# Scheduler constants of a fused attention and feed-forward kernel, judged by replays with varied lengths instead of the one undisturbed plan

## The chip, the cores and the metric

The kernel runs on one core of a Trainium2 chip. The metric is the device time of one execution in microseconds (us), lower is better. A core has a matrix engine (PE), three engines for elementwise work (DVE, ACT and POOL), and DMA queues; SP issues the transfers here. Each engine works through its own list of instructions in the order in which the program wrote them, and waits where an operand is not ready.

## The reference

Three stages are computed one after another, for 4 batches of 544 tokens and 512 channels:

```
# attention: 8 heads of 64, 512 local tokens and 32 global ones
out_g = softmax(scale * q_g @ [k_g k_l].T) @ [v_g v_l]
s_ll  = where(|i - j| <= 32, scale * q_l @ k_l.T, -1e9)
out_l = softmax([scale * q_l @ k_g.T, s_ll]) @ [v_g v_l]
x = concat(out_g, out_l)                     # (4, 544, 512)
# first feed-forward, 1024 wide
h = relu(x @ w_in)
conv[t] = sum over k of conv_w[k] * h[t + k - 1]     # 3 taps along the tokens
x = (h * sigmoid(conv)) @ w_out
# second feed-forward, 1024 wide
xk = mu_k * x + (1 - mu_k) * x_prev;  xr = mu_r * x + (1 - mu_r) * x_prev
out = sigmoid(xr @ w_r) * (relu(xk @ w_k) ** 2 @ w_v)
```

All data is float32. In the feed-forwards the kernel splits each operand into a high and a low part and makes three products of it (high by high, high by low, low by high).

## The kernel before

**Tiles.** Attention is cut into 16 units u (a batch and a pair of heads). A unit has scores `s` (L541, 32 small matmuls for each of its two heads), a masking pass on DVE that makes `e` (L556), the exponentials on ACT (L563), a transposition `pe` on PE (L572), its copy `eT` (L575), the product with v, `o` (L582), a division on DVE (L592 to L594, tile `xn`), a transposition `X` (L613) and the split into a high and a low `x` (L620, L623). For the global tokens two units go together: `sg` (L665), exponentials `eg` (L682), the normalising of `eg` (fnorm: L697 on ACT, L701 on POOL), the transpositions `peg` (L709), their copies `egT` (L714), the product `Xg` (L724) and its split into `x` (the high part by ACT at L750, the low part by DVE at L753).

The first feed-forward of batch b has two parts, called H and O here. H makes `ph` (L905) in 8 blocks of 128 channels by two halves of the tokens, 12 matmuls each; the first 6 of the 12 need the x of the batch's first two units, the last 6 those of its last two (`x_2`, `x_3` in batch 0). Each block of 128 channels then goes through relu, three taps `c` (L940 to L947), the sigmoid (L953, ACT), the multiplication by h (L956, DVE or POOL) and the split into `gh` (L963) and `gl` (L968). O makes `po` (L1006); its blocks of k come in four pairs, and a pair needs `gh` and `gl` of two blocks of channels: `c_6` and `c_7` are the last pair. The second feed-forward (called moe2 here, with `pk`, `pr` and `pv` on PE) runs in 6 chunks of up to 384 tokens after the last O; its squaring is at L1166.

**What sets the order.** The program first lists all its work as tasks (class Plan), each with an engine, a cost in nanoseconds, its dependencies, the buffers that it takes, and for some a due time, called key. `schedule()` then plays the program through once and writes the instructions in the order that comes out. Of the tasks that can start within WINDOW of the earliest, on the engine of that one, it takes the one with the smallest key. A task that several engines can do goes to the engine with the earliest modelled end, plus a bias for the engine that depends on the modelled time (`bias`, with PHASES as the borders and DVE_BIAS, ACT_BIAS, POOL_BIAS as the values, L386). PENALTY is added to the key of an ACT task that needs another table of functions, AHEAD bounds the bytes under way in DMA, and the FILL constants say where the PE is given empty matmuls (L429) to bridge a wait. The due times come from s_key (L497: T_START and STEP0 for batch 0, T_DENSE, SLOT, LEAD, GAP, GAP1 for the later ones), from the LAG constants (how far behind its unit's start a unit's `pe`, `o`, `X` and `peg` are due), and from d_key (L867: T_DENSE, SLOT, H_FRAC for H and O).

Of the kernel before, what the change touches and what calls it, by code (L numbers as in the profile page):

```python
# [45 lines left out]
W2R_BUFS = 3  # L46
E_STEP = 16
XB = 8
T_START = 3947
STEP0 = 4107  # L50
T_DENSE = 30229
SLOT = 69882
LEAD = -9653
GAP = -8788
GAP1 = 13075
STEPS_H = 6
E_BUFS = 4
H_FRAC = 0.625
LAG_TE = -2476
LAG_PV = 14647  # L60
LAG_G = 12072
LEAD_Q = 6126
S_COST = 880
M_COST = 845
E_COST = 1182
PV_COST = 470
LAG_TX = 18273
WINDOW = 90
FILL_MIN = 31
FILL_MARGIN = 1350  # L70
FILL_START = 6
FILL_RATE = 0.504
PENALTY = 496
AHEAD = 1711
PHASES = (60e3, 105e3, 320e3, 375e3)
DVE_BIAS = (1137, 1116, 682, -803, 690)
ACT_BIAS = (604, 900, -279, 1717, 327)
POOL_BIAS = (914, 623, 302, -621, -2645)
H_BUFS = 5
C_BUFS = 3  # L80
G_BUFS = 4
# [80 lines left out]
class Plan:  # L162
# [50 lines left out]
    def schedule(self):  # L213
# [17 lines left out]
        while cand:  # L231
# [39 lines left out]
            for e, t, o in ests:  # L271
                if o[0] == o0[0] and e <= lim:
                    k = t.key + (PENALTY if t.table and t.table != table else 0)
                    if best is None or k < best[0]:
# [20 lines left out]
            if t.eng == "PE":  # L295
# [4 lines left out]
                unit = 215 / r  # L300
                if t.warm and e - now > FILL_MIN + FILL_MARGIN:
                    n = int((e - now - FILL_MARGIN) / unit)
                    t.fill += n
                    clock.run(now, 215 * n, 1.0, True)
                if t.warm and r == 1.0:
                    left = (k + 1) * Clock.TICK - e
                    lack = Clock.ENOUGH - clock.count.get(k, 0.0) - FILL_RATE * left
                    if lack > 0:
                        n = min(int(lack / (1 - FILL_RATE) / 215) + 1, int(left / 215))
                        t.fill += n  # L310
# [93 lines left out]
def attn_moe_kernel(  # L404
# [92 lines left out]
    def s_key(u):  # L497
        b, s = divmod(u, NP)
        if b == 0:
            return T_START + STEP0 * s  # L500
        g0, gh, g1 = (GAP1 if b == 1 else GAP), H_FRAC * SLOT, SLOT - LEAD
        return T_DENSE + SLOT * (b - 1) + g0 + (g1 - g0) * s / NP

# [23 lines left out]
    def attend(u):  # L527
# [22 lines left out]
        for a in range(2):  # L550
# [36 lines left out]
            def fdiv(a=a, bo=bo):  # L587
                if a == 0:
# [11 lines left out]
            e = add("ACT", E_COST, fe, deps=[m], use=[be], table="exp", name=f"e{u}_{a}")  # L600
            t = add("PE", 437, ft, deps=[e], take=[bp, bt], use=[be], key=k0 + LAG_TE + 1500 * a,
                    name=f"te{u}_{a}", warm=True)
            te = add("ACT", act(512), lambda fev=fev: fev(nc.scalar.copy), deps=[t], use=[bt, bp],
                     name=f"tev{u}_{a}", alts=[("DVE", 600, lambda fev=fev: fev(nc.vector.tensor_copy))])
            pv = add("PE", PV_COST, fpv, deps=[te, ev["v", u]], take=[bo], use=[bt, bufs["v", u]],
                     key=k0 + LAG_PV + 1500 * a, name=f"pv{u}_{a}", warm=True)
            dvs.append(add("DVE", 740, fdiv, deps=[pv] + dvs, take=[bn] if a == 0 else [],
# [6 lines left out]

        tx = add("PE", 437, ftx, deps=dvs, take=[bX], use=[bn], key=k0 + LAG_TX + 1500, name=f"tx{u}")

# [28 lines left out]
    def glob(u):  # L645
# [70 lines left out]
        def fpv():  # L716
            X = alloc(bt[2], [P, 2, SG], F32, f"Xg{u}")
            eT = bT.tile
            for z in range(2):
# [15 lines left out]
                alts=[("ACT", 710, lambda: fnorm(nc.scalar)), ("POOL", 858, lambda: fnorm(nc.gpsimd))])  # L735
        kt = k0 + LAG_G
        evs = []
# [129 lines left out]
    def d_key(b, pos):  # L867
        hp = FT * h_cost
        t0 = T_DENSE + SLOT * b
        if b == B - 1:  # L870
            return t0 + pos
        if pos < hp:
            return t0 + SLOT * H_FRAC * pos / hp
        return t0 + SLOT * (H_FRAC + (1 - H_FRAC) * (pos - hp) / hp)

# [178 lines left out]
    def moe2():  # L1054
        t0 = T_DENSE + SLOT * (B - 1) + 2 * FT * h_cost
        free_out = add("-", 0, alloc_big, deps=[ev["O", B - 1, m, hf] for m in range(KT) for hf in range(2)],
# [234 lines left out]
    wout, wout_done = split_weights("wout", w_out, FT, DM, lambda: woutp, "wo", ("gh", "gl"))  # L1291
    add("DMA", 900, fmus, key=T_DENSE + SLOT * 2, name="mus")
    for b in range(B):
# [113 lines left out]
```

## Time and profile before

| | |
|---|---|
| median of 3 runs | 549.32 us (548.07 to 549.88) |
| the profiled execution | 551.77 us, of which the span of the trace is 550.0 us |
| mean granted clock of PE | 0.988 of full speed |
| busy in the span | PE 528.0, DVE 320.8, ACT 287.0, POOL 155.4 us |

The span runs from the first to the last recorded instruction; the rest of the time lies around it. An engine is busy while one of its instructions runs. PE's two clock levels are 1.2 and 2.4 GHz; a granted clock of 1.00 is the upper one, 0.50 the lower, and a value between them is a mean over a stretch that had both.

### The profile page before, as it was taken

To read this page: it belongs to the slowest core of one execution; us is meant where nothing else is said; L and a number is where in the kernel's file an instruction comes from. 1 tells how busy PE (TensorE), PEld (TensorE's weight loads), DVE (VectorE), ACT (ScalarE), POOL (GpSimd) and SP (SyncE) were. 2 spreads that over 40 slices of the span, in tenths; PEclk is the share of its full clock that TensorE was granted. 3 is DMA by queue.
4 is the path that set the end of the run, shared out by engine and by line. 5 is a ranking of instruction groups with operands and counts; after the bars stand their busy time and mean duration, and the time that the engine had idled before them with its cause. 6 is when DMAs were issued, how large, how long until landed. Compare 5 with 4: busy or idle time off the path is not lost.

```text
span 550.0 us, 13792 instructions
## 1 busy us (share of the span) xinstructions
PE 528.0 (96%) x5498; PEld 483.9 (88%) x5498; DVE 320.8 (58%) x874; ACT 287.0 (52%) x638; POOL 155.4 (28%) x320
## 2 busy tenths in 40 slices
PE   5688989999999999999999999999999999999997
PEld 4576979978999999999999998898898898898896
DVE  4489899176796349942599689998115215111101
ACT  5588988366798559973696574001042142142040
POOL 3053243101021112210100372000089288184060
PEclk9699998999999999999999999999999999999999
DMA  8998854887154670010427532302101100100101
GB/s 262 306 285 287 288 180 152 220 278 246 62 195 124 211 227 6 2 39 25 136 80 216 166 116 72 116 0 59 57 2 38 68 0 21 57 1 0 59 1 38
DMA packets 41088, 64.60 MB, mean 117 GB/s; under 512 B 4928, under 2 KB 31296, under 8 KB 41024
## 3 DMA queue, kind: packets, MB, share of 16 engines
q1 hardware_dynamic: 38720, 59.26, 34.0%
q10 hardware_dynamic: 2304, 4.47, 2.2%
q8 instruction: 43, 0.70, 0.5%
q14 instruction: 21, 0.17, 0.1%
HBM read 51.64 MB, written 12.07 MB: 116 GB/s over the span
## 4 chain that ended last, share of the span: by engine, by line
PE 72%; ACT 1%; DVE 1%; issue 0%
PE pk L1143 17%; PE pv L1246 17%; PE po L1006 13%; PE ph L905 10%; PE pr L1209 9%; PE o L582 1%; PE Xg L724 1%; PE pe L572 1%; PE s L541 1%; PE X L613 1%; PE sg L665 1%; PE peg L709 0%; DVE c L947 0%; ACT c L940 0%; ACT gh L963 0%
## 5 line engine op out<-in xcount | busy, mean ns | idle before, releaser
L905 PE MATMUL ph<-x,win_hi 128*128 128x256 f32 (+1 forms) x512 | 100.4, 294 | 1.3 <-ACT egT L714 0.8
L905 PEld LDWEIGHTS ph<-x,win_hi 128*128 128x128 f32 x512 | 79.9, 188 | 2.9 <-ACT egT L714 1.1
L1006 PE MATMUL po<-gh,wout_hi 128*128 128x256 f32 (+1 forms) x256 | 75.5, 295 | 0.0
L1006 PE MATMUL po<-gl,wout_hi 128*128 128x256 f32 (+1 forms) x256 | 73.9, 289 | 0.1
L1006 PE MATMUL po<-gh,wout_lo 128*128 128x256 f32 (+1 forms) x256 | 73.4, 287 | 0.0
L905 PE MATMUL ph<-x,win_lo 128*128 128x256 f32 (+1 forms) x256 | 73.4, 287 | 0.0
L1143 PE MATMUL pk<-xkl,wkk_hi 128*128 128x384 f32 (+1 forms) x192 | 62.7, 327 | 0.0
L1143 PE MATMUL pk<-xkh,wkk_lo 128*128 128x384 f32 (+1 forms) x192 | 62.7, 327 | 0.0
L1143 PE MATMUL pk<-xkh,wkk_hi 128*128 128x384 f32 (+1 forms) x192 | 62.7, 326 | 0.0
L1166 POOL TENSOR_TENSOR robuf<-robuf 128x384 f32<-128x384 f32 (+1 forms) x40 | 32.9, 824 | 103.1 <-ACT robuf L1161 102.9
L947 DVE SCALAR_TENSOR_TENSOR c<-h,convw,c 128x544 f32<-128x544 f32 x64 | 50.5, 808 | 14.3 <-ACT c L940 12.3
L1246 PE MATMUL pv<-wvv_lo,k2h 128*128 128x512 f32 (+1 forms) x144 | 54.4, 378 | 0.0
L1246 PE MATMUL pv<-wvv_hi,k2h 128*128 128x512 f32 (+1 forms) x144 | 54.4, 378 | 0.0
L1246 PE MATMUL pv<-wvv_hi,k2l 128*128 128x512 f32 (+1 forms) x144 | 54.4, 377 | 0.0
L1161 ACT ACTIVATE robuf<-pk 128x384 f32<-128x384 f32 (+1 forms) x40 | 18.7, 467 | 65.2 <-PE pk L1143 64.5
L1259 DVE TENSOR_TENSOR robuf<-pv,robuf 128x512 f32<-128x512 f32 (+1 forms) x18 | 11.9, 661 | 65.7 <-PE pv L1246 56.6
L1006 PEld LDWEIGHTS po<-gh,wout_hi 128*128 128x128 f32 x256 | 48.2, 188 | 0.3
L1006 PEld LDWEIGHTS po<-gl,wout_hi 128*128 128x128 f32 x256 | 48.2, 188 | 0.3 <-DVE gl L968 0.3
L905 PEld LDWEIGHTS ph<-x,win_lo 128*128 128x128 f32 x256 | 48.2, 188 | 0.0
L1006 PEld LDWEIGHTS po<-gh,wout_lo 128*128 128x128 f32 x256 | 48.2, 188 | 0.0
L563 ACT ACTIVATE e<-e 128x128 f32<-128x128 f32 x128 | 40.2, 390 | 8.4 <-DVE e L556 8.3
L1209 PE MATMUL pr<-wrr_hi,xrbuf 128*128 128x512 f32 x136 | 43.7, 395 | 0.0
(194 smaller groups left out, 1120.6 us busy)
## 6 DMA issues: line engine op xcount, KB each, us to landing
v<-in_v_l_dram SPq DMA_DIRECT2D x16, 910.0 KB, 7.0
kT<-in_k_l_dram SPq DMA_DIRECT2D x16, 336.0 KB, 4.7
qT<-in_q_l_dram SPq DMA_DIRECT2D x16, 288.0 KB, 4.3
x2d<-xo ACTq DMA_DIRECT2D x16, 272.5 KB, 3.5
out_dram<-robuf SPq DMA_DIRECT2D x16, 256.0 KB, 2.0
wout_0r<-in_moe_w_out_dram SPq DMA_DIRECT2D x8, 256.0 KB, 3.8
wkk<-wkkd SPq DMA_DIRECT2D x8, 256.0 KB, 2.9
wout_0r<-in_moe_w_out_dram SPq DMA_DIRECT2D x8, 255.8 KB, 4.3
```

The costliest lines, as they stand in the source:

```text
L541: nc.tensor.matmul(s[a][32 * j : 32 * j + 32, i], lhsT=qT[rows[a], q : q + 32], rhs=kT[rows[a], c : c + P], start=(i == 0), stop=True, ski ...
L563: nc.scalar.activation(be.tile[:, P * i : P * (i + 1)], be.tile[:, P * i : P * (i + 1)], AF.Exp, bias=be.tile[:, SL + i : SL + i + 1], sca ...
L572: nc.tensor.transpose(pt[:, i], be.tile[:, P * i : P * (i + 1)], ident)
L905: nc.tensor.matmul(pm, lhsT=w[:, k, P * m : P * (m + 1)], rhs=x[:, s0:s1], start=(k == 0 and n == 0), stop=(k == KT - 1 and n == 2),)
L947: e.scalar_tensor_tensor(bc.tile, bh.tile[:, k : k + S], convw[:, FT * k + m : FT * k + m + 1], bc.tile, op0=ALU.mult, op1=ALU.add,)
L1006: nc.tensor.matmul(pm, lhsT=w[:, k, P * m : P * (m + 1)], rhs=g[:, k % 2, s0:s1], start=(k == 0 and n == 0), stop=(k == FT - 1 and n == 2),)
L1143: nc.tensor.matmul(bp.tile[:, :n], lhsT=w[:, k, P * m : P * (m + 1)], rhs=x[:, :n], start=(k == 0 and i == 0), stop=(k == KT - 1 and i == 2),)
L1161: e.activation(kk()[:, :n], bp.tile[:, :n], AF.Relu)
L1166: e.tensor_mul(ks()[:, :n], kk()[:, :n], kk()[:, :n])
L1209: nc.tensor.matmul(bp.tile, lhsT=x[:, P * j : P * (j + 1)], rhs=w[:, k], start=(k == 0 and i == 0), stop=(k == KT - 1 and i == 2),)
L1246: nc.tensor.matmul(bp.tile, lhsT=x, rhs=w[:, k, c0:c1], start=(k == 0 and i == 0), stop=(k == FT - 1 and i == 2),)
L1259: nc.vector.tensor_mul(o()[:, c0:c1], bp.tile, r()[:, c0:c1])
```

## The change

Only numbers are changed: the constants above get new values. The functions that use them, the tasks, their costs and their dependencies stay as they were. The new values were picked by a search that replays each order with varied lengths of the tasks; the old ones had been picked by the single plan that `schedule()` makes.

```diff
-T_START = 3947
-T_DENSE = 30229
+T_START = -1763
+T_DENSE = 17832
...
-LAG_PV = 14647
-LAG_G = 12072
+LAG_PV = 43495
+LAG_G = 2385
...
-PENALTY = 496
+PENALTY = 1220
-PHASES = (60e3, 105e3, 320e3, 375e3)
-DVE_BIAS = (1137, 1116, 682, -803, 690)
+PHASES = (45588, 264400, 484313, 683508)
+DVE_BIAS = (1064, 1001, -4113, 2464, 14683)
```

The same lines change in the same manner for STEP0, SLOT, LEAD, GAP, GAP1, H_FRAC, LAG_TE, LEAD_Q, LAG_TX, FILL_MIN, FILL_MARGIN, FILL_RATE, AHEAD, ACT_BIAS and POOL_BIAS.

**What it does to the program.** The matmuls are the same ones, in another order, but for one empty matmul that is no longer there. Of the tasks that have a choice of engine, these change theirs: 14 of the 32 multiplications by h go from DVE to POOL, all but one of them in batches 1 to 3; 32 of the 48 squarings of moe2 go from POOL to DVE, with 24 of its subtractions for the low part of the square; 12 low parts of weights (win and the weight wvv of moe2) go from POOL to DVE. The orders of PE and of the queue of loads are the same up to the first 46 rows of PE. After that the q and k of units 4 to 6 are loaded ahead of the last two tiles of w_in (columns 512 and up, k of 2 and 3).

On ACT, ahead of the high parts of `x_2` and `x_3` that the second half of batch 0's H needs, there stood before:

```order
L790 CAST convm<-convr 128x24
L843 CAST win_hi<-win_512m 128x512
L714 COPY egT_858<-peg_1_904 128x384
L563 ACTIVATE e_0_912<-e_0_912 128x128 x4
L790 CAST wout_0m<-wout_0r 128x512
L563 ACTIVATE e_1_964<-e_1_964 128x128 x4
L750 CAST x_2_166<-Xg_969 128x32
L750 CAST x_3_168<-Xg_969 128x32
```

And now, on the same engine and at the same place:

```order
L790 CAST convm<-convr 128x24
L843 CAST win_hi<-win_512m 128x512 x2
L563 ACTIVATE e_1_955<-e_1_955 128x128 x4
L790 CAST wout_0m<-wout_0r 128x512
L563 ACTIVATE e_0_980<-e_0_980 128x128 x4
L563 ACTIVATE e_1_986<-e_1_986 128x128 x4
L843 CAST wout_hi<-wout_0m 128x512
L682 ACTIVATE eg_1029<-sg_0_968,eg_1029 128x480
L682 ACTIVATE eg_1029<-sg_1_969,eg_1029 128x64
L750 CAST x_2_166<-Xg_998 128x32
L750 CAST x_3_168<-Xg_998 128x32
```

Counted from ACT's first row, two more sets of exponentials of a unit (`e`, one of them ahead of the rows shown), one more cast of wout, one more copy `eT` and the exponentials of the next pair's global tokens (`eg`) now stand ahead of the two casts.

The normalising of batch 1's first `eg` stood on ACT, behind three sigmoids of batch 0's gate:

```order
L575 COPY eT_0_1409<-pe_0_1388 128x512
L953 ACT_TABLE_LOAD
L953 ACTIVATE c_4_1359<-c_4_1359 128x544
L953 ACTIVATE c_3_1375<-c_3_1375 128x544
L953 ACTIVATE c_6_1399<-c_6_1399 128x544
L697 ACTIVATE eg_1063<-eg_1063 128x608
L963 CAST gh_4_1508<-c_4_1359 128x544
```

It stands on POOL now, among the clearings of the buffers for wout and ahead of the first h of batch 0:

```order
L785 MEMSET wout_0m 128x512
L525 MEMSET v_951 128x28
L672 MEMSET eg_1029 128x64
L785 MEMSET wout_0m 128x512 x2
L701 TENSOR_SCALAR eg_1029<-eg_1029 128x608
L785 MEMSET wout_0m 128x512
L925 MEMSET h_0_1096 128x1
```

So it comes before all sigmoids, on another engine.

Around the sigmoid of `c_7`, the last block that batch 0's O waits for, ACT had this order:

```order
L714 COPY egT_1525<-peg_1_1593 128x384
L953 ACTIVATE c_5_1591<-c_5_1591 128x544
L953 ACTIVATE c_7_1599<-c_7_1599 128x544
L790 CAST ewkk_0m<-ewkk_0r 128x256
L563 ACT_TABLE_LOAD
L563 ACTIVATE e_0_1631<-e_0_1631 128x128 x4
```

Now it has this one:

```order
L953 ACTIVATE c_5_1482<-c_5_1482 128x544
L714 COPY egT_1504<-peg_1_1565 128x384
L563 ACT_TABLE_LOAD
L563 ACTIVATE e_0_1596<-e_0_1596 128x128 x4
L953 ACT_TABLE_LOAD
L953 ACTIVATE c_7_1570<-c_7_1570 128x544
L750 CAST x_4_172<-Xg_1620 128x32
L750 CAST x_5_174<-Xg_1620 128x32
```

A set of exponentials, with a load of the table for them and one back, has moved in between the two sigmoids. On PE, batch 0's O now has all four groups of `po` on its third pair, and then the scores of two units, ahead of the first `po` on the last pair; before, it had two groups and the scores of one unit there, and the scores of the other unit came after O.

## Rows read from the trace of the kernel before

**Rows 1.** The page, part 1 (busy us, share, instructions) and part 2 (40 slices).

```profile
PE 528.0 (96%) x5498; PEld 483.9 (88%) x5498; DVE 320.8 (58%) x874; ACT 287.0 (52%) x638; POOL 155.4 (28%) x320
...
PEclk9699998999999999999999999999999999999999
```

**Rows 2.** Windows: stretch, length, busy PE PEld DVE ACT POOL, PEclk, DMA share, GB/s.

```profile
40.00:74.00 34.00, 31.78 (x392) 29.52 (x391) 30.73 (x84) 31.86 (x71) 7.74 (x26) 1.00 0.91 301
...
151.00:311.50 160.50, 160.28 (x1966) 155.05 (x1966) 112.30 (x310) 114.60 (x238) 21.59 (x82) 1.00 0.38 117
311.50:550.00 238.50, 235.16 (x1213) 210.59 (x1211) 101.18 (x196) 63.92 (x146) 96.42 (x120) 1.00 0.14 44
```

**Rows 3.** The chain that ended last, in order of time, two pieces of batch 3.

```profile
263.11 24.31 PE ph L905 x192
287.42 24.11 PE po L1006 x192
```

**Rows 4.** Timeline of PE at batch 0's second half of H (start, us).

```profile
50.17 0.63 PE L572 MATMUL pe<-ident,e 128*128 128x128 f32 x4 [0.29 <-DVE e L556]
...
52.68 0.50 PE L905 MATMUL ph<-x,win_hi 128*128 128x256 f32 x2
```

**Rows 5.** Timeline of ACT ahead of that point.

```profile
46.12 0.22 ACT L790 CAST convm<-convr 128x24 f16<-128x24 bf16 x1 [1.54 <-POOL v L525]
...
47.13 1.28 ACT L563 ACTIVATE e<-e 128x128 f32<-128x128 f32 x4
...
50.11 0.25 ACT L750 CAST x<-Xg 128x32 fp32r<-128x32 f32 x2
50.66 0.62 ACT L843 CAST wout_hi<-wout_0m 128x512 fp32r<-128x512 f32 x1 [0.30 <-DVE wout_0m L794]
```

**Rows 6.** Timeline of DVE at the same point.

```profile
51.39 0.27 DVE L753 TENSOR_TENSOR x<-Xg,x 128x32 fp32r<-128x32 f32 x2
```

**Rows 7.** Timeline of PE in batch 0's O.

```profile
81.81 0.55 PE L709 MATMUL peg<-ident,eg 128*128 128x128 f32 x3 [1.91 <-ACT eg L697]
...
91.04 1.16 PE L541 MATMUL s<-kT,qT 64*32 64x128 f32 x64
...
92.54 0.36 PE L1006 MATMUL po<-gh,wout_hi 128*128 128x256 f32 x1
```

**Rows 8.** Windows in batch 0's O and right behind it (columns as in rows 2).

```profile
82.00:87.00 5.00, 5.00 (x111) 4.11 (x111) 4.70 (x10) 4.03 (x8) 2.10 (x3) 0.66 0.34 110
100.00:104.00 4.00, 4.00 (x34) 4.00 (x33) 0.00 (x0) 0.00 (x0) 0.00 (x0) 1.00 0.80 232
```

**Rows 9.** Timeline of ACT in batch 0's O.

```profile
80.97 0.79 ACT L697 ACTIVATE eg<-eg 128x608 f32<-128x608 f32 x1
...
87.81 1.36 ACT L953 ACTIVATE c<-c 128x544 f32<-128x544 f32 x2 [0.72 <-DVE c L947]
...
89.57 1.28 ACT L563 ACT_TABLE_LOAD   x1
```

**Rows 10.** Timeline of POOL in batch 0's O.

```profile
88.61 2.25 POOL L956 TENSOR_TENSOR c<-c,h 128x544 f32<-128x544 f32 x2 [2.55 <-ACT c L953]
```

**Rows 11.** Timeline of DVE in batch 0's O.

```profile
90.82 0.79 DVE L963 CAST gh<-c 128x544 fp32r<-128x544 f32 x2
91.52 1.35 DVE L968 TENSOR_TENSOR gl<-c,gh 128x544 fp32r<-128x544 f32 x2
```

**Rows 12.** Timeline of PE in batch 1's attention and first H.

```profile
115.45 1.84 PE L572 MATMUL pe<-ident,e 128*128 128x128 f32 x8
...
126.44 0.53 PE L905 MATMUL ph<-x,win_hi 128*128 128x288 f32 x2 [0.82 <-ACT egT L714]
```

**Rows 13.** Timeline of DVE, the division behind an `o` (last operation).

```profile
37.93 0.42 DVE L594 TENSOR_TENSOR xn<-o,xn 128x256 f32<-128x256 f32 x1
```

**Rows 14.** A group of DVE by line and form (busy, mean ns, idle before).

```profile
L1166 DVE TENSOR_TENSOR robuf<-robuf 128x384 f32<-128x384 f32 x8 | 4.5, 557 | 0.2
```

More of the change, by code (lines that the diff above doesn't have):

```diff
@@ L48 @@
 XB = 8
-T_START = 3947
-STEP0 = 4107
-T_DENSE = 30229
[L52 to L55, printed above, removed]
+T_START = -1763
+STEP0 = 4043
+T_DENSE = 17832
+SLOT = 73969
+LEAD = -12026
+GAP = -1608
+GAP1 = 16095
 STEPS_H = 6
 E_BUFS = 4
-H_FRAC = 0.625
-LAG_TE = -2476
-LAG_PV = 14647
-LAG_G = 12072
-LEAD_Q = 6126
+H_FRAC = 0.649
+LAG_TE = -2867
+LAG_PV = 43495
+LAG_G = 2385
+LEAD_Q = 2184
 S_COST = 880
@@ L66 @@
 PV_COST = 470
-LAG_TX = 18273
+LAG_TX = 30701
 WINDOW = 90
-FILL_MIN = 31
-FILL_MARGIN = 1350
+FILL_MIN = 695
+FILL_MARGIN = 3342
 FILL_START = 6
-FILL_RATE = 0.504
-PENALTY = 496
-AHEAD = 1711
-PHASES = (60e3, 105e3, 320e3, 375e3)
-DVE_BIAS = (1137, 1116, 682, -803, 690)
-ACT_BIAS = (604, 900, -279, 1717, 327)
-POOL_BIAS = (914, 623, 302, -621, -2645)
+FILL_RATE = 0.433
+PENALTY = 1220
+AHEAD = 1768
+PHASES = (45588, 264400, 484313, 683508)
+DVE_BIAS = (1064, 1001, -4113, 2464, 14683)
+ACT_BIAS = (490, 169, -8356, -6555, -2690)
+POOL_BIAS = (4492, 476, -3056, -5498, 6560)
 H_BUFS = 5
```

## The prediction

> **What bounds the kernel now.** I read the page first. PE is busy in 528.0 of 550.0 us, and the work of PE is the same before and after but for one empty matmul [rows 1]. So the end can move only by the time that PE loses: where it waits, and where its clock is granted at the lower level. The row of the granted clock shows where to look: it falls below the highest digit in some slices of the first 110 us and nowhere behind them [rows 1].
>
> Next I cut the span into windows. From 151.0 to 311.5 PE is busy in 160.28 of 160.5 us at a clock of 1.00: nothing is to be gained there, only lost. From 311.5 to the end it is busy in 235.16 of 238.5, and DVE in 101.18 [rows 2]. The chain of waits in order of time agrees: a whole H takes 24.31 us and a whole O 24.11, each 192 matmuls back to back, 0.126 us apiece [rows 3]. That leaves the front. The order of PE and of the loads is unchanged over the first 46 rows of PE, so what is lost before some 31 us stays lost. From 40 to 74 us PE has 2.2 us of idle time, and its feeders are nearly full: DVE is busy in 30.73 and ACT in 31.86 of 34 us [rows 2]. There, in batch 0's O, and in batch 1's attention the change can do something. I take these places in order of time. All sums are made against the profiled execution (551.77 us, span 550.0), which lies 2.45 us above the median of 549.32; I apply the difference to the median.
>
> **Place 1, batch 0's second half of H: +1.3 us.** Before, PE began it at 52.68 [rows 4]. Its inputs are two casts by ACT that began at 50.11 and ended at 50.36 [rows 5], and two subtractions by DVE behind them, which ended at 51.39 + 0.27 = 51.66 [rows 6]. So the inputs were there 1.02 us before PE came. Now ACT has more ahead of the two casts: two sets of exponentials of 1.28 busy each, one cast of wout of 0.62 [rows 5], and the exponentials of `eg`, 544 columns in two instructions, which by the 512 columns of a set I put at 1.1. That is 4.3 by busy times; neighbours overlap by about 0.1 at each seam (the casts that began at 50.11 were ended 0.30 before the next began at 50.66), so I count 3.9. The copy `eT` and what else moved I put into ACT's remaining idle time: 34 less 31.86 is 2.1, of which 1.54 is one wait, ahead of the cast of the conv weights [rows 2, 5], and 0.6 is left. That wait of 1.54 goes too, because the cast stands behind more work now. So the inputs come 3.9 − 1.54 = 2.4 later, PE's slack of 1.02 takes its part, and 1.3 is left: H's second half begins near 54.0. Bounds: if all 2.1 of idle time, and the 0.30 at 50.66, are filled, 3.9 − 2.4 − 1.0 = +0.5; if none is, because the loads are late, 3.9 − 1.0 = +2.9. The loads: q and k of units 4 to 6, 1.25 MB, go ahead of two tiles of w_in, which at the 301 GB/s of that stretch [rows 2] makes these some 4.1 us late. The tiles themselves are needed only 72 matmuls (9 us) into the second half, which hides that; without the cover the 4.1 us would stand in H. Of the 12 low parts of weights that go from POOL to DVE, four are w_in's and fall here; DVE's own idle time of 3.3 us [rows 2] is their cover, and if it did not hold, the low parts of x would be late by as much as ACT's and not on top of it.
>
> **Place 2, batch 0's O: −2.6 us.** Before, PE waited 1.91 us for ACT's normalising of `eg`, until 81.81 [rows 7]. ACT had it behind three sigmoids, at 80.97 [rows 9]. Right after, PE's mean clock from 82 to 87 was 0.66 [rows 8]: 3.4 of the 5 us at the lower level, where half of the work is lost, 1.7 us. The normalising is now on POOL and far ahead, so 1.91 + 1.7 = 3.6 can be saved. Against this stands the last pair of O. Before, the sigmoid of `c_7` ended at 87.81 + 1.36 = 89.17, POOL's multiplication at 90.86 [rows 9, 10], `gh` and `gl` on DVE at 91.52 + 1.35 = 92.87 [rows 11], while PE came at 92.54 [rows 7]: just in time. Now two loads of tables (1.28 each [rows 9]) and a set of exponentials (1.2) stand ahead of that sigmoid, 3.8 us; the normalising that left ACT gives back 0.8. The sigmoid ends near 92.2, and with a multiplication of 1.12, a `gh` of 0.4, a `gl` of 0.68 and half a microsecond of hand-overs the pair is there at 94.9. When does PE come? Before it took 92.54 − 52.68 = 39.9, of which 3.6 are the loss above: 36.3. Now 12 more `po` (1.5) and one more block of scores (1.16 [rows 7]) stand ahead of the pair; the four transpositions more and four fewer that go with them cancel. So 54.0 + 36.3 + 2.7 = 92.9 or so. The wait is at most about 2.0, and none if `c_5` and `c_7` come earlier through H, whose order also changed. I take half, 1.0, and 2.6 of the 3.6 are saved. Bounds: −3.6 without a wait, and +0.1 if the wait of 2.0 is followed by the same 1.7 us of low clock.
>
> **Place 3, batch 1's attention: −0.9 us.** Eight transpositions took 1.84 us where four back to back are 0.44, so 0.96 is a pause within them, and PE waited 0.82 at 126.44 for a copy [rows 12]: 1.8 together. The scores of the third unit now stand inside O, so its exponentials can run around 100 us, where DVE, ACT and POOL have no work at all [rows 8]. I take half; bounds 0 and −1.8.
>
> **Place 4, the start of the third H: +0.4 us.** A transposition `X` now stands six `po` (0.75 us) behind its `o`. Between them lies DVE's division, whose largest operation is 0.42 [rows 13]; with two small ones ahead and two hand-overs it is about 1.1. Bounds 0 and +1.0.
>
> **The rest, 0.** The 13 multiplications that go to POOL in batches 1 to 3 lie where DVE is busy in 112.30 of 160.5, ACT in 114.60 and POOL in 21.59, and PE never waits [rows 2]; without that cover a multiplication on POOL costs 0.4 us more than one on DVE. In moe2 DVE gets 32 squarings of 0.557 [rows 14] and 24 subtractions of the like, about 31 us on 101.18 of 238.5 [rows 2]: 133, still far below PE. Bounds 0 and +1.0 (a chunk that starts with one of these).
>
> **The sum**: 1.3 − 2.6 − 0.9 + 0.4 = −1.8. The span would be 548.2 and the median 549.32 − 1.8 = **547.5 us**. 0.3%, about what a measurement here can tell from no change, is 1.65 us.
>
> **Rivals.**
>
> *A larger gain.* No wait for the last pair, all of place 3, the low bound at place 1: 0.5 − 3.6 − 1.8 = −4.9, 544.4 us. For it speaks that DVE has less ahead of `c_7`; against it that place 1 is late by ACT's plain work.
>
> *The low clock moves to place 1.* In the trace a wait of 1.91 us at 79.9 was followed by 3.4 us at a granted clock of half [rows 7, 8]. Now the last transposition of `e` ahead of H's second half ends near 50.80 as before [rows 4] (the scores of `sg`, which stood behind it, have moved ahead of it and end by then if their inputs let them), and H goes on at 54.0: a pause of up to 3 us, longer than the one that was followed by the low clock. That costs 1.7 once more: −0.1, 549.2 us. The Trainium skill ("TensorE: Matmul & The Clock Gate", Part 1, The HAM clock gate) says that the throttled clock is the default and activity releases it; by that rule this pause costs a stretch of half clock just as the other did, and the sum would be this rival's. The trace bears it out at 82 us; at 50 us, with a pause of 0.29 [rows 4], the clock stayed at 1.00 [rows 2].
>
> *Slower: ACT's queue.* If ACT is late by all that was put ahead of H's second half (+2.9), `c_7` is late with it; the pair's wait then comes in full with its low clock (+0.1), nothing is won at place 3, and +0.4 stays: +3.4, 552.7 us. It decides from the point where the casts of `x_2` and `x_3` end after 54 us. For it speaks that ACT is the fuller of the two feeders, against it that much of that work could start earlier than its old place.
>
> *The terms cancel otherwise* (place 3 not won, the pair's wait in full without the low clock): 1.3 − 1.6 + 0.4 = +0.1, 549.4 us.
>
> **Chances.** The forecast, −1.7 to −4, 0.32; the larger gain 0.13: faster 0.45. The low clock at place 1 0.20 and the terms that cancel 0.12: same 0.32. Slower 0.23. Forecast and larger gain start at 543.5; of the slower cases the upper part, above 551.5, is left out with some 0.1, and below 543.5 another 0.08. The forecast's own range is 545.3 to 547.6.
>
> **What the changed profile would show.** Right: `ph` on `x_2` begins near 54.0 and ACT's two casts end near 52.7; the wait of 1.91 for the normalising is gone and the granted clock from 80 to 88 is 1.00; the wait for the last pair is below 2 us; less idle time between 115 and 128; windows from 151 on as full as before. Wrong: a granted clock near 0.5 right behind 54 us, a wait ahead of the last pair that is followed by one, new waits in batches 1 to 3 for POOL's multiplications, or gaps of PE in moe2 behind DVE.

## The result and the profile after

The change makes the kernel slower: 552.66 us median of 10 runs, against 548.54 for the kernel before in 10 runs beside them. The ratio is 1.0078, with a 95% interval of 1.0055 to 1.0101, so some 4.3 us (3.0 to 5.5). The forecast of 547.5 us had the wrong sign, and its range ended at 551.5. The profiled execution took 553.6 us, with a span of 551.8.

The page of the changed kernel, parts 1 and 2 (to be held against [rows 1]):

```profile
PE 525.0 (95%) x5496; PEld 483.1 (88%) x5496; DVE 330.5 (60%) x911; ACT 306.3 (56%) x678; POOL 84.3 (15%) x241
...
PEclk9798999999999999999999999999999999999999
```

POOL has lost almost half of its work and ACT and DVE have it, on average with much room. Averages don't show where it hurts; windows of the changed kernel do (columns as in [rows 2]):

```profile
40.00:74.00 34.00, 26.41 (x319) 24.25 (x304) 25.77 (x73) 28.55 (x67) 10.13 (x29) 0.90 0.90 300
46.00:50.40 4.40, 2.01 (x53) 1.87 (x54) 3.42 (x25) 2.12 (x6) 0.58 (x2) 1.00 1.02 329
50.40:51.20 0.80, 0.80 (x4) 0.44 (x3) 0.51 (x1) 0.80 (x4) 0.00 (x0) 0.51 0.75 235
54.00:58.00 4.00, 3.83 (x20) 3.83 (x21) 2.24 (x7) 2.95 (x11) 1.85 (x7) 0.59 0.78 265
...
151.00:311.50 160.50, 159.87 (x2079) 154.66 (x2079) 113.89 (x294) 112.56 (x234) 29.97 (x89) 1.00 0.37 115
313.50:552.00 238.50, 235.03 (x1213) 210.45 (x1211) 113.14 (x244) 82.94 (x184) 17.08 (x31) 1.00 0.14 44
```

From 151 on PE is as full as it was, and moe2 takes the same time although DVE has 113.14 us of work in it where it had 101.18 [rows 2]. What is lost is lost ahead of that: in the first window PE is busy in 26.41 of 34 us, where it was 31.78, and the granted clock is 0.90. The clock falls at 50.4: up to there it is 1.00, though from 46.0 on PE is busy in only 2.01 of 4.40 us, and right behind it is 0.51. The timeline of PE in the changed kernel shows at which instructions (start, duration, instruction, and in brackets the idle time ahead of it with what ended it):

```profile
43.03 1.16 PE L541 MATMUL s<-kT,qT 64*32 64x128 f32 x64 [1.49 <-ACT egT L714]
...
46.50 0.34 PE L665 MATMUL sg<-kT,qT 128*64 128x64 f32 x4 [1.23 <-DVE e L556]
48.72 1.59 PE L724 MATMUL Xg<-egT,v 96*64 96x32 f32 x48 [1.89 <-DVE e L556]
...
54.17 1.11 PE L572 MATMUL pe<-ident,e 128*128 128x128 f32 x4 [2.93 <-ACT eg L682]
54.94 0.77 PE L905 MATMUL ph<-x,win_hi 128*128 128x256 f32 x2
...
78.48 0.39 PE L1006 MATMUL po<-gl,wout_hi 128*128 128x256 f32 x1 [0.68 <-DVE gl L968]
...
95.62 1.95 PE L541 MATMUL s<-kT,qT 64*32 64x128 f32 x119
99.81 0.43 PE L541 MATMUL s<-kT,qT 64*32 64x128 f32 x9 [2.24 <-issue]
100.16 0.39 PE L1006 MATMUL po<-gh,wout_hi 128*128 128x256 f32 x1
...
128.98 1.24 PE L724 MATMUL Xg<-egT,v 96*64 96x32 f32 x36 [1.08 <-ACT egT L714]
```

The second half of batch 0's H begins at 54.94 (before 52.68 [rows 4]). The wait of 1.91 us for the normalising [rows 7] is gone, as predicted. New are waits of 1.49, 1.23 and 1.89 us between 41 and 49, a pause of 2.93 us ahead of that H, one of 2.24 us inside a block of scores, and a wait at 128.98 for the copy that PE had waited 0.82 us for [rows 12]. The waits of 1.23 and 1.89 belong to one change of PE's order: the scores `sg` of the next pair, which stood behind the transpositions `pe`, now stand ahead of `Xg`, and both wait there for DVE's `e`, the pass that reads the scores before them.

### The profile page after: what moved, and what is told of

It is laid out like the page before. It is cut to its first block, busy times and chain, and to the rows that moved or that the text cites. A ratio compares the mean times of both kernels' runs of the same rounds, so it can differ in the third digit from the quotient of the medians.

```text
span 551.8 us, 13735 instructions
## 1 busy us (share of the span) xinstructions
PE 525.0 (95%) x5496; PEld 483.1 (88%) x5496; DVE 330.5 (60%) x911; ACT 306.3 (56%) x678; POOL 84.3 (15%) x241
## 4 chain that ended last, share of the span: by engine, by line
PE 77%; DVE 4%; DMA 3%; ACT 2%; issue 1%; POOL 1%; ACTq 0%; DVEq 0%; SPq 0%; POOLq 0%
PE pk L1143 17%; PE pv L1246 17%; PE po L1006 15%; PE ph L905 11%; PE pr L1209 9%; PE s L541 2%; PE Xg L724 2%; PE o L582 2%; PE pe L572 1%; DVE c L947 1%; DMA ewkk_0r<-in_moe_w_k_dram 1%; DMA wkkd<-ewkk_768m 1%; DMA ewkk_512r<-in_moe_w_k_dram 1%; PE X L613 1%; DMA wkkd<-ewkk_256m 1%
## 5 line engine op out<-in xcount | busy, mean ns | idle before, releaser
L905 PE MATMUL ph<-x,win_lo 128*128 128x288 f32 (+1 forms) x256 | 73.8, 288 | 0.0
L1161 ACT ACTIVATE robuf<-pk 128x384 f32<-128x384 f32 (+1 forms) x48 | 22.7, 473 | 74.8 <-PE pk L1143 74.7
L947 DVE SCALAR_TENSOR_TENSOR c<-h,convw,c 128x544 f32<-128x544 f32 x64 | 53.1, 844 | 11.9 <-ACT c L940 9.6
L956 POOL TENSOR_TENSOR c<-c,h 128x544 f32<-128x544 f32 x23 | 27.8, 1214 | 66.2 <-ACT c L953 66.2
```

The source lines that it names most:

```text
L905: nc.tensor.matmul(pm, lhsT=w[:, k, P * m : P * (m + 1)], rhs=x[:, s0:s1], start=(k == 0 and n == 0), stop=(k == KT - 1 and n == 2),)
L947: e.scalar_tensor_tensor(bc.tile, bh.tile[:, k : k + S], convw[:, FT * k + m : FT * k + m + 1], bc.tile, op0=ALU.mult, op1=ALU.add,)
L956: e.tensor_mul(bc.tile, bc.tile, bh.tile[:, 1 : S + 1])
L1161: e.activation(kk()[:, :n], bp.tile[:, :n], AF.Relu)
```

## The experiments

Ratios are to the kernel before, run on the same chip beside each kernel. In the diffs, `put(names, behind)` takes tasks out of the finished order and puts them right behind another task, and `fn = opts[0]` or `opts[1]` sets a task's operation to its form for ACT or DVE (`opts[2]`, for the normalising, to the one for POOL). A line of dots stands for lines left out of a diff: those that set behind which transfer a moved load may start. No kernel here leaves out work.

**Each kernel looked at twice more.** The first question was whether one profile of each is enough. Both were run again unchanged, two executions of each with a profile.

> The kernel before, unchanged, for a second profile. Single executions of one kernel have differed by 5 to 8 us so far, more than the two kernels do, so the places have to be compared over several profiles. Theory A: the spread arises in the first 33 us (loads and clock), and from the first global product to the second half of H batch 0 takes 16.6 to 16.9 us as in both profiles of this order so far. Rival B: the spread arises everywhere, and the two profiles so far agree by chance.

> The kernel before once more, as its second profile: theory A has the span follow the time at which the first global product starts, within 1.5 us; rival B has it not follow.

> The changed kernel, unchanged, for a second profile. Theory A (the loss is at fixed places): from the first global product to the second half of batch 0's H takes 20 us or more, against 17 in the kernel before, and the pause of 2.2 us inside the second of two blocks of scores stands ahead of O's last pair again. Rival B: either is gone, and was an accident of one execution.

> The changed kernel once more: theory A has the second half of H at 20 us or more behind the first global product and the pause between the scores at 2 us; rival B has at least one of them away.

They took 546.71 and 547.95 us (before), 556.96 and 555.73 us (after). The timeline of PE in the first of these executions of the kernel before:

```profile
51.86 0.50 PE L905 MATMUL ph<-x,win_hi 128*128 128x256 f32 x2
...
74.75 0.38 PE L1006 MATMUL po<-gl,wout_hi 128*128 128x256 f32 x1 [0.63 <-DVE gl L968]
...
79.84 0.55 PE L709 MATMUL peg<-ident,eg 128*128 128x128 f32 x3 [0.20 <-ACT eg L697]
```

And in the second:

```profile
52.20 0.50 PE L905 MATMUL ph<-x,win_hi 128*128 128x256 f32 x2
...
80.19 0.55 PE L709 MATMUL peg<-ident,eg 128*128 128x128 f32 x3 [0.21 <-ACT eg L697]
```

From the first `Xg` to H's second half it took 17.4 and 16.2 us in the kernel before (16.6 to 16.9 had been expected) and 19.7 and 19.8 in the changed one (20 or more). The span did not follow the start of that `Xg`: 35.83, 34.44 and 36.02 us go with spans of 550.0, 544.9 and 546.2.

In neither execution of the kernel before does PE wait 1.91 us for the normalising: it waits 0.20 and 0.21, and the clock stays up. The 3.6 us that the forecast wanted to save at its place 2 were an accident of the one execution that was read. The new pauses are no accident as a whole, though each varies. Here is the window from 40 to 140 us of the first of those two executions of the kernel before:

```profile
40.00:140.00 100.00, 97.40 (x1465) 90.44 (x1465) 76.12 (x246) 79.21 (x183) 23.11 (x77) 0.99 0.73 236
```

The same window of the second:

```profile
40.00:140.00 100.00, 95.92 (x1459) 88.40 (x1458) 75.89 (x244) 78.45 (x181) 23.12 (x77) 1.00 0.72 237
```

And the same window of the changed kernel in its second execution:

```profile
40.00:140.00 100.00, 90.06 (x1376) 83.46 (x1376) 69.38 (x224) 73.46 (x172) 24.63 (x71) 0.93 0.71 228
```

The third:

```profile
40.00:140.00 100.00, 91.16 (x1382) 85.04 (x1382) 69.07 (x225) 74.51 (x175) 24.13 (x71) 0.93 0.70 226
```

PE is idle some 5 to 7 us longer and runs at a granted clock of 0.93 where it was 0.99 to 1.00. The starts of batch 0's second H and of moe2 cut the span in three. That H begins at 52.25 on average over the three executions of before and at 54.93 after: +2.7. From there to moe2 it is 256.3 (254.6 to 258.9) and 260.4 (258.6 to 261.8): +4.1. Moe2 itself is the same. The sum of 6.8 is above the 4.3 us of the medians because all three profiled executions of the changed kernel were above its median: their spans are 551.8, 555.2 and 554.0, and the median of 552.66, less the 1.8 us outside the span, is 550.9.

Two of the new waits come every time: those for DVE's `e` at `sg` (1.11 to 1.24 us) and at `Xg` (1.88 or 1.89) stand in all eleven profiles of the changed order and its variants, and ahead of `Xg` in none of the nine of the old order. In all eleven the granted clock falls around them, between 46 and 51 us, and stays down for 3.4 to 10.2 us. No experiment here put `sg` back, so what this costs is not shown.

**The normalising on POOL, alone, in the kernel before.** This takes the one part of the change that the forecast counted as its gain.

```diff
+put(["gi5", "gn5"], "gl0_1")
+task["gn5"].fn = task["gn5"].opts[2][2]
```

> The kernel before with the normalising of batch 1's first eg, and the two small operations of DVE ahead of it, put before three taps of the convolution and onto POOL: the part of the change from which the prediction took its gain, alone. Theory A (prediction, place 2): PE's wait of 1.91 at 79.9 and the 3.4 us of half clock behind it go, 3.6 us, 545 where the kernel before has 548.5. Rival B: the pause goes, but PE then comes earlier to the next transposition or to the last pair and waits there (PE came just in time for that pair): between -0.5 and -2 us.

548.96 us, 1.0022 (0.9992 to 1.0051): no gain. The timeline of PE:

```profile
78.82 0.52 PE L709 MATMUL peg<-ident,eg 128*128 128x128 f32 x3 [1.08 <-DVE xn L592]
```

Counted from H's second half, the transposition begins at 28.9 us, against 29.1, 28.0 and 28.0 in the three executions of the kernel before; PE now waits there for an operation of DVE on `xn`. The first theory, that the change wins place 2 and loses it elsewhere, falls: there was next to nothing to win.

**Scores apart.** In the changed order two blocks of 64 score matmuls stand behind each other in batch 0's O. Here the second goes 24 `po` further back, as in the order before.

```diff
+put(["s8"], "O0_1_1.3")
+put(["m8_0"], "s8")
```

> The changed kernel with the scores of the second of the two units that stand back to back ahead of O's last pair put 24 matmuls of that pair later. Theory A (PE's pause of 2.24 us inside the second of these two blocks, which the profile puts to no wait, is PE getting its instructions: two blocks of 64 small matmuls in a row use them up faster than they are fetched): the pause is gone, and the time falls by about 2.2 us against the changed kernel, to 550.4. Rival B (PE waits there for the last pair or for a buffer): the pause stands at the same time, ahead of the last pair, and the time stays within 0.7 us.

549.93 us, 1.0038 (1.0008 to 1.0067): it takes back about half of the loss. The two blocks run without a pause:

```profile
94.55 1.16 PE L541 MATMUL s<-kT,qT 64*32 64x128 f32 x64
...
98.85 1.16 PE L541 MATMUL s<-kT,qT 64*32 64x128 f32 x64
```

What stopped PE in the changed kernel has no semaphore: the releaser is "issue", in the middle of a block. The view of the DMA queues from 95.0 to 97.5 us says what else went on (packets, MB, time as a share of the 16 engines'):

```profile
q1 hardware_dynamic: 526, 0.94, 101.2%
```

And from 97.5 to 100.0:

```profile
q1 hardware_dynamic: 308, 0.43, 51.7%
q8 instruction: 1, 0.02, 2.5%
```

Queue q8 is taken to be that of PE's instructions: its 43 packets of 16 KB are 64 bytes for each of PE's 10,992 recorded operations, weight loads included. Its only packet in this stretch was on its way from 97.58 to 98.56, PE stood still from 97.57 to 99.81, and loads of v and of tiles of w_k had filled all DMA engines until then. The same pause is 1.67 us in the second execution, ahead of the very same matmul, where the packet landed at 97.15 and PE stood from 97.10 to 98.78; it is missing in the third, where all 128 matmuls take 2.06 us and the packet had landed 1.99 us before PE came to that matmul. With the scores apart it had landed 2.69 us before, with the DMA engines as full (103.8% from 92.0 to 95.6 us). That the scores' place costs the pause is shown, and the rows tie it to the packet (the last section has more of them); that the packet was late because of the loads is argued, for no run took the loads away.

The converse, the two blocks together in the kernel before:

```diff
+put(["s7"], "s8")
```

> The kernel before with the scores of a second unit put right behind those of another in batch 0's O, as the changed kernel has them. Theory A (two blocks of 64 small matmuls in a row outrun the fetching of PE's instructions): a pause of 1.5 to 2.5 us appears inside or right behind the second block that no wait explains, and 549 to 550 where the kernel before has 547.5. Rival B (the pause belongs to what else is ready there): no such pause, and a time within 0.7 us.

551.66 us, 1.0076 (1.0047 to 1.0104), some 4 us. The timeline of PE in it:

```profile
91.98 1.08 PE L541 MATMUL s<-kT,qT 64*32 64x128 f32 x56 [2.44 <-DVE e L556]
```

The window of this kernel from there on:

```profile
92.00:97.00 5.00, 5.00 (x76) 4.80 (x77) 1.91 (x12) 1.93 (x7) 0.30 (x3) 0.66 0.65 234
```

Here the pause has another releaser: the second block waits for DVE's `e`, the operation that reads scores. Then comes a stretch at 0.66. So the neighbours cost time in either order, but not by one mechanism.

**ACT's cast of wout, later.** In the changed kernel the timeline of ACT ahead of batch 0's second H reads:

```profile
49.88 0.77 ACT L790 CAST wout_0m<-wout_0r 128x512 f16<-128x512 bf16 x1 [2.28 <-DMA wout_0r<-in_moe_w_out_dram]
50.52 2.44 ACT L563 ACTIVATE e<-e 128x128 f32<-128x128 f32 x8
...
54.31 0.26 ACT L750 CAST x<-Xg 128x32 fp32r<-128x32 f32 x2
```

The cast waits 2.28 us for its load, and two sets of exponentials, those of `eg` and the casts of `x_2` and `x_3` stand behind it. The first run moves the cast and its three successors behind the next pair's `eg`; the second joins this with the scores apart.

```diff
+put(["abswout0_0", "lowwout0_0", "hiwout0_0", "lowout0_0"], "gi5")
```

> The changed kernel with one thing put elsewhere: the four operations on the first tile of wout (cast on ACT, low bits on DVE, high and low part) stand behind the split of batch 0's second global product instead of ahead of two sets of exponentials. Theory A (the cast waits 2.3 us for its load at the head of ACT's list and holds up everything behind it): ACT's wait of 2.28 at 49.9 is gone, H's second half begins near 52.5 instead of 54.94, the pause of 2.9 us ahead of it shrinks below 1 us and with it the stretch of half clock at 54 to 57: 2.4 + up to 1.2 us, 549 to 550.5 where the changed kernel has 552.7. Rival B (ACT's plain amount of work is what is late, not the wait): the second half begins at 54 or later, and the time stays within 1 us of the changed kernel's.

> The changed kernel with both moves, the first wout tile later and the two blocks of scores apart. If both theories hold, their gains add, since the places lie 40 us apart with PE never idle for long between them: 552.7 - 3.5 - 2.2 = 547.0, which is 1.5 us below the kernel before. If the gains do not add (the time won at the first place is waited away at the last pair, whose c_7 is not earlier): 549 to 550.

553.14 us, 1.0115 (1.007 to 1.0159), and 553.99 us, 1.0116 (1.0077 to 1.0155). H's second half begins at 51.10 in the first, 3.8 us earlier (3.3 counted from batch 0's fourth block of scores), and nothing is won. The timeline of PE in that first one:

```profile
77.08 0.58 PE L1006 MATMUL po<-gl,wout_hi 128*128 128x256 f32 x1 [3.10 <-DVE gl L968]
```

The window of the same kernel around it:

```profile
76.00:83.00 7.00, 5.92 (x36) 5.57 (x40) 5.02 (x7) 4.62 (x10) 3.56 (x5) 0.51 0.12 39
```

What PE gained it now waits for at O's fifth `po`, the first that needs the low part of the second of the first pair's two blocks: that pair of gated blocks is not there sooner. A limit that neither theory had named holds batch 0 together.

**What makes O's first pair late?** Counted from batch 0's fourth block of scores, that `po` begins 56.8, 57.6 and 56.8 us later in the three executions of the kernel before and 56.0 in its variant with POOL, but 60.8, 59.1 and 61.6 in those of the changed kernel (where PE waits for it 0.68, 0 and 2.39 us) and 59.9 in its variant with the later cast. The timeline of ACT shows the delay on its way, in the sigmoids of the first three blocks. In the kernel before:

```profile
64.59 0.66 ACT L953 ACTIVATE c<-c 128x544 f32<-128x544 f32 x1
...
66.25 0.66 ACT L953 ACTIVATE c<-c 128x544 f32<-128x544 f32 x1
```

In the changed kernel:

```profile
64.91 0.66 ACT L953 ACTIVATE c<-c 128x544 f32<-128x544 f32 x1
...
71.06 0.67 ACT L953 ACTIVATE c<-c 128x544 f32<-128x544 f32 x1
```

The first of them is that of the pair's first block and the third that of its second. Between them ACT had two operations of relu besides a sigmoid; now it has eleven others, among them two casts of wout and two first taps. No run put this order of ACT back. Two suspects were tested: the load of v of unit 5 (910 KB), now ahead of wout's tiles, and eight operations that went from DVE to ACT in that stretch (three casts for wout, three relu, two copies). First each is undone in the changed kernel, alone and with the scores apart, and then both.

```diff
 # wout first
+put(["ldwout1_0", "ldwout2_0", "ldwout3_0", "ldv5"], "ldwout0_0")
+put(["one5"], "zerowout4_0")
 ...
 # eight on DVE
+for n in ["hiwout1_0", "hiwout4_0", "hiwout6_0", "relu0_6_0",
+          "relu0_6_1", "relu0_5_0", "tev4_1", "tev5_1"]:
+    task[n].fn = task[n].opts[1][2]
```

> The changed kernel with the loads of three tiles of wout ahead of the load of v for unit 5 (910 KB), and the clearing of that v later on POOL. Theory A (ACT's cast of wout waits for its load because v's load shares the queues with it, and in order behind it stand the exponentials and the split that H's second half needs; moving the cast alone only put the wait at O's first pair, because wout's later casts then held up the relu of H): the cast's wait is below 0.5 us, H's second half begins within 35 us of the fourth block of scores (37.2, 36.2 and 36.5 in the three profiles of the changed kernel, 33.9 to 34.8 in those of the kernel before), no wait for gl above 1 us follows at O's first pair, and the time falls by 1.5 to 3 us from 552.7. Rival B (ACT's plain work): the wait goes, but the second half still begins 36 us or more behind, and the time stays within 1 us.

> The same, and the two blocks of scores apart as in the earlier run that gave 549.9. Theory A: both gains add to 547 to 548, the level of the kernel before (547.5 on that chip); this would account for the whole loss. Rival B: 549.5 or more, some loss is elsewhere.

> The changed kernel with eight operations of batch 0's H back on DVE, where the kernel before has them: three high parts of wout, three relu, two copies eT (1.3 + 1.2 + 1.3 us of DVE for about 4.0 of ACT); nothing is moved. Theory A (ACT is the engine that is too full in H: from 64 to 72 us it is busy in 7.99 of 8 us there, and DVE waits for it, 7.3 us in all between 46 and 80, against 2.1 in the kernel before): DVE's waits for ACT halve, gl of O's first pair is there 2 to 4 us earlier counted from the fourth block of scores (60 to 61.6 us now, 56 to 57.8 in the kernel before), and the time falls by 1.5 to 3 us from 552.7. Rival B (wout's late loads are what is late in H): gl stays within 1 us of where it is, and so does the time.

> The same eight operations back on DVE, and the two blocks of scores apart (549.9 alone). Theory A: the two places account for the loss, so 547 to 548.5, the level of the kernel before (547.5 to 548.5). Rival B: no better than 549.5.

> The changed kernel with three things set back together: six of wout's loads ahead of v of unit 5 and of q and k (as the kernel before has them), the eight operations on DVE, and the two blocks of scores apart. Theory A (loads and engine choice make the first pair of O late only together: with either alone the other still holds it up): gl of that pair within 58 us of the fourth block of scores, and a time at the level of the kernel before, 547 to 549. Rival B (it is the order of the operations on ACT and DVE in H that is worse): gl at 60 or later and 550 or more.

Wout first: 554.14 us, 1.0117 (1.0074 to 1.0161), and with the scores apart 552.0, 1.0071 (1.0045 to 1.0098). Eight on DVE: 554.75, 1.0134 (1.0105 to 1.0163), and with the scores apart 551.41, 1.0058 (1.0036 to 1.008). All three, with all of wout's first seven tiles ahead of v: 554.99, 1.0131 (1.01 to 1.0162). Neither suspect, undone here, gives anything back; the scores apart help each time (by 0.45% and 0.75%; only together with the later cast they did not). The timeline of ACT with wout first shows why:

```profile
46.67 0.76 ACT L790 CAST wout_0m<-wout_0r 128x512 f16<-128x512 bf16 x1 [0.53 <-DMA wout_0r<-in_moe_w_out_dram]
...
58.96 0.78 ACT L790 CAST wout_0m<-wout_0r 128x512 f16<-128x512 bf16 x1 [3.93 <-DMA wout_0r<-in_moe_w_out_dram]
```

The wait of 2.28 has moved: 0.53 us for the first tile, 3.93 for a later one. With all three it is 6.02 us at wout's last tile. With the eight on DVE, the list of ACT's waits from 46 to 80 us has one that has grown from 1.0 us in the changed kernel (us in total, times, longest):

```profile
ACT c L940 <- DVE gl L968: 3.8, 2, 2.5
```

So in these rows one part put back alone makes another wait longer.

**The same suspects, added to the kernel before.** There the surroundings are the old ones.

```diff
 # eight on ACT: as above with opts[0]
 # v early
+put(["ldv5"], "ldwout0_0")
 ...
 # scores together
+put(["s7"], "s8")
```

> The converse: the kernel before with the same eight operations put on ACT, nothing moved. Theory A: gl of O's first pair comes 2 to 4 us later, PE waits for it 2 us or more where it waits 0.6, and the time rises by 1.5 to 4 us. Rival B: no more than 0.7 us, DVE and ACT are exchangeable there.

> The kernel before with the load of v for unit 5 (910 KB) right behind the first tile of wout, where the changed kernel has it, nothing else moved: the converse for the loads. Theory A: ACT's casts of wout then wait for their loads, 2 us or more in all, gl of O's first pair comes 1 to 3 us later, and the time rises by 1 to 3 us. Rival B: within 0.7 us, the loads have slack in this order.

> The kernel before with both things that make O's first pair late there: the load of v early (alone +1.3 us) and the eight operations on ACT (alone +2.1). Theory A (both hold up the same pair, which came 60.6 us behind the fourth block of scores with either, so they overlap): 1.5 to 2.8 us above the kernel before. Rival B (they add): 3 us or more, with the pair at 62 or later.

> The kernel before with all three: the early load, the eight operations on ACT, and two blocks of scores in a row (alone +3.8). Theory A (these three are what the changed order costs): at least the 4.1 us by which the changed kernel is slower, 4 to 6.5. Rival B (a delay of the first pair gives the fetch the time that the scores use up, so they do not add): 2.5 to 4.

| Added to the kernel before | us | ratio (95%) | loss, us (of 548) |
|---|---|---|---|
| eight on ACT | 550.28 | 1.0039 (1.0019 to 1.006) | 2.1 |
| v early | 549.21 | 1.0025 (1.0001 to 1.0049) | 1.4 |
| both | 552.16 | 1.0091 (1.0057 to 1.0126) | 5.0 |
| both, and scores together | 558.25 | 1.018 (1.0139 to 1.0221) | 9.9 |

Each of the first two alone brings the wait that the changed kernel's variants show. PE with the eight on ACT:

```profile
79.25 0.39 PE L1006 MATMUL po<-gl,wout_hi 128*128 128x256 f32 x1 [1.65 <-DVE gl L968]
```

And with v early:

```profile
77.63 0.39 PE L1006 MATMUL po<-gl,wout_hi 128*128 128x256 f32 x1 [2.30 <-DVE gl L968]
```

Against the distance of 56 to 57.6 us, both have 60.6. So each of the three parts costs time by itself (v early only just clear of the noise). The expectation by which the first two overlap (1.5 to 2.8 us) fell, with 5.0; for all three both expectations did (2.5 to 4, and 4 to 6.5), with 9.9. Together the three cost more than twice what the whole change does: either the changed order wins some 5 us back, by rows that no experiment here has picked out, or these parts cost less among its other rows.

## Why the prediction was wrong

**Place 2 (−2.6) is the step that failed.** It took 3.6 us as there to be saved: a wait of 1.91 and the half clock behind it, both read from one execution. They stand in one of three executions of the kernel before; the other two have 0.2 us there, so what was there to be saved was an accident of the execution read. Putting the normalising on POOL alone gave 1.0022 instead of a gain. The wait of 1.0 for the last pair that was set against it did not come in this form: the sigmoid of `c_7` ended at 91.74 + 0.66 = 92.40, near the 92.2 that was worked out. That is in part luck, since the working left out that a later H makes `c_7` later too: counted from H's second half the sigmoid came 1.0 us later than before, not the 3.0 that had been added, and that half itself 2.3 later. PE came to the last pair at 100.16 and did not wait, where 92.9 had been worked out. One reading was wrong there. The `po` at 92.54 is the first on the third pair; 12 of them stand ahead of the last pair, which began, in the kernel before, at

```profile
94.14 0.27 PE L1006 MATMUL po<-gh,wout_hi 128*128 128x256 f32 x1
```

So PE had come 1.3 us behind that pair's input and not just in time, and the same working gives 94.6 for its coming now and a wait of 0.3 for what was put at 2.0. Of the 5.6 us from there to 100.16, 0.9 is the later H, 2.24 the pause of PE inside the scores, 0.68 the wait for the first pair, and some 1.1 the half clock at H's start. That pause was not foreseen; the two blocks of scores in a row were counted at 1.16 us more and no wait. It is the second missing term, worth 0.40% (some 2.2 us) by the run with the scores apart.

**Place 1 (+1.3) was of the right sign and too small**: H's second half begins at 54.94 in the profiled execution, 2.3 us later than before, and 2.7 on average, against the upper bound of +2.9. The mechanism was the one named, ACT's queue, but what filled it was a load: 2.28 us at the cast of wout, whose tile was assumed to be there. The scores `sg`, which were to cost nothing ahead of `Xg` if their inputs let them, did not get them in time: 1.23 us there and 1.89 at `Xg`. The rival of the low clock came true in the place that it named, 54 to 58 us at 0.59, but not by its mechanism. It had the clock fall behind the pause of up to 3 us; the clock fell at 50.4, before that pause (2.93 us, from 51.24 on) had begun, behind a stretch in which PE was busy in 2.01 of 4.40 us. The rule of the Trainium skill that was weighed there ("TensorE: Matmul & The Clock Gate", Part 1, The HAM clock gate), that the throttled clock is the default and activity releases it, agrees in kind with these rows.

But a cure of place 1 alone is worth nothing, as the run with the later cast showed. **The prediction missed that O's first pair is nearly late already**: PE waited 0.63 and 0.64 us for it in the two repeats of the kernel before. Its estimate of when PE comes to O's end (36.3 us behind H, plus 2.7) had the last pair as the only input in question. In the changed kernel PE comes to that `po` 3.4 us later on average, counted from the scores, and an earlier H only makes that wait longer, 3.1 us, with half clock behind it. The rival "ACT's queue" had the price nearly right (552.7 us against 552.66) with its condition met, since the casts of `x_2` ended at 54.57; but it put the wait at the last pair, where there was none, and had no pause in the scores, so the price was luck.

**Place 3 (−0.9) went the other way.** PE waits for the copy `egT` ahead of `Xg` for 1.08, 2.81 and 1.86 us in the three executions, and in the last two of these PE's clock is down afterwards. The timeline of PE in the second execution:

```profile
129.61 2.14 PE L724 MATMUL Xg<-egT,v 96*64 96x32 f32 x36 [2.81 <-ACT egT L714]
```

The window from there on:

```profile
129.00:136.00 7.00, 6.39 (x138) 5.77 (x139) 4.23 (x22) 2.14 (x7) 0.76 (x6) 0.55 0.68 207
```

**Place 4 (+0.4)** was not isolated. **The rest (0) was right**: the rows from 151 on and of moe2 are the same within 0.5 us, with 13 multiplications on POOL and DVE at 113.14 us in moe2, where 133 had been estimated. The list of tasks that change their engine, on which that estimate went, was not whole: in moe2 another 36 operations go from DVE to ACT, and the eight in batch 0's H were not on it either.

**What stays open.** Which part of the order on ACT and DVE makes the first pair late in the changed kernel is not settled: undoing the load's place, the eight operations, or both, gains nothing there, though each costs time in the old order. Not tested is ACT's order between the first and the third sigmoid, nor `sg` ahead of `Xg`. Also open is whether the changed order wins some 5 us back elsewhere. No version beat the kernel before; the best one of the changed kernel is the one with the scores apart, at 1.0038.

## What to carry to other kernels

A wait in one profiled execution is worth counting as a gain only when a second and third execution show it too: here the largest term was gone in both. A stretch in which all feeders are full has a next late input behind each one that is cured, so cost a gain by the time of that next input (here O's first pair) and not by the wait that it removes. On an engine that works in order, look at what a cast waits for before counting only its own time, since everything behind it waits for that load as well.

## What the runs showed of the hardware

Executions of one program differ by up to 7 us: the kernel before took 544.9 to 552.14 us in 23 executions on one chip.

PE stopped within a block of 128 score matmuls of which nothing in the program held back the rest, for 2.24 and 1.67 us in two of three executions, both times ahead of the same one. Such pauses, without a releaser in the profile, fall at fixed places: in the twenty traces there are 57 of more than 0.15 us. Of these 53 ended 1.2 to 1.6 us after a 16 KB packet of queue q8 had landed, and they stand at seven places of PE's list, between which lie 125 to 127 matmuls or a multiple of that (each with its weight load; a packet has 256 times 64 bytes). The kernel before has them too, 1.60 us inside its first `Xg` in the second execution. That such a packet is late when loads fill the DMA engines (101.2% in the 2.5 us before the pause of 2.24) is argued and not shown.

Not every pause of PE is followed by the lower clock. With 3.10, 2.81 and 2.44 us the granted clock fell (0.51, 0.55, 0.66 in the windows shown), behind 2.24 us in the changed kernel (100 to 106 us) and 1.65 us in the kernel with eight on ACT (79 to 86 us) it stayed at 1.00, and behind 1.91 in the kernel before [rows 7, 8] it fell. In the changed kernel it fell ahead of the pause of 2.93 us. The length of a pause alone doesn't decide here, and what a fall costs differs: 3.4 of 5 us were at the lower level in the kernel before, but 6.3 of the 7 us from 129 on in the changed kernel's second execution. So a sum that adds 1.7 us for each such pause is neither a bound nor a price.
